# Local attention heads from the third chunk on: two at a time in plain float32 in place of one at a time with split operands

## The chip, the cores and the metric

The kernel runs on one core of a Trainium2 chip. TensorE (PE, with its weight loads as PEld) multiplies matrices, VectorE (DVE), ScalarE (ACT) and GpSimd (POOL) work on elements, SyncE (SP) issues transfers. The metric is the device time of one execution in microseconds, as a median over runs.

## The reference

Eight batches of eight heads, 576 positions, head size 64. Heads 0 to 3 attend to the last 32 positions, heads 4 to 7 to positions of the same remainder modulo 32. The result, heads side by side, goes through two dense layers with a squared ReLU between them. All of it is float32.

```python
def _attn_ref(q, k, v) -> np.ndarray:
    ...
    scores = scale * np.matmul(q, k.transpose(0, 1, 3, 2))
    ...
    mask_local = (rel >= 0) & (rel < stride)
    mask_strided = (rel >= 0) & (pos[None, :] % stride == pos[:, None] % stride)
    ...
    scores = np.where(masks[None, :, :, :], scores, -1000000000.0)
    scores = scores - np.max(scores, axis=-1, keepdims=True)
    attn = np.exp(scores)
    attn = attn / (np.sum(attn, axis=-1, keepdims=True) + 1e-09)
    return np.matmul(attn, v).astype(np.float32)

def _moe_ref(x, w_in, w_out) -> np.ndarray:
    h = np.maximum(x @ w_in, 0.0)
    return (h * h @ w_out).astype(np.float32)
```

Here x is 4608 x 512, `w_in` 512 x 2048 and `w_out` 2048 x 512.

## The kernel before

**Chunks and the MLP.** The 4608 tokens go in 12 chunks of 384. In each chunk the MLP runs over 16 tiles of the hidden dimension (slots). `up` (L466) does twelve matmuls of 384 columns per slot (L476), ScalarE applies ReLU, square and a rounding to `gh`, VectorE makes the remainder `gl` (L490). `down` (L494) does nine matmuls of 512 columns per slot (L509) into three PSUM banks, two slots later than `up`. The MLP's operands are split: a value is a rounded part (`float32r`, one instruction a matmul) and the remainder that the rounding left, and three of the four products are summed. That split is what all names with `h`/`l`, `x` or two halves stand for.

**Attention of the next chunk.** While the MLP of chunk c runs, the attention of chunk c+1 is done beside it. The strided heads (`strided`, L401) are products on GpSimd and sums on VectorE, with no TensorE. The local heads use TensorE. The first two chunks (`NPLAIN`, chunks 0 and 1) do them in pairs with `pe_pair` (L295) in plain float32: scores at L325 with 64 rows for each head, head 0 on partitions 0 to 63 and head 1 on 64 to 127; output at L381 with 64 output partitions for each head. Chunk 1's pairs lie among chunk 0's MLP matmuls. From the third chunk on, `pe_head` (L199) does one head at a time:

- loads: queries and keys, twice over on 128 partitions (L214), and values (L215);
- splits: rounded keys and queries on ScalarE (L220, L222), remainders on GpSimd (L221, L223);
- scores: four windows of 96 queries by 128 keys, one matmul of 256 columns each (L237), a column for a key and one for its remainder; the remainder's half and the mask are added on VectorE (L241), and the minimum is taken with the other half (L229);
- exponentials with row sums on ScalarE (L246), reciprocals on VectorE (L247, L248), scaling on ScalarE (L251) or, for the last head, on GpSimd (L254);
- probabilities transposed in blocks of 32 on VectorE into `p_t` (L262) and split (L270 to L272), values split (L257, L258);
- output: four matmuls of 192 columns on 128 x 128 weights (L283), whose parts are summed on ScalarE and VectorE (L286 to L288), then split into the MLP's operands `xlh` and `xll` (L290, L291).

PSUM banks 3 and 4 are taken in turn for scores and outputs.

**What sets the order.** TensorE's order is written out. For every two slots (a step, `j // 2` from 0 to 7) `plan[step]` (L569) names the heads that go one stage on before the two `up`s, between `up`s and `down`s, and after them; `take` (L580) advances the generators, and ties the matmuls behind the last ones with `issue_after`. The loads for the head 0 and 1 of a chunk and the split of head 0 come at slot 14 of the chunk before (L689). On the other engines and in SP's queue of transfers a scheduler orders the instructions by its own simulated times, with the program's order as the priority. A tile of a pool with `bufs=1` is written only when the tile before it in that place is no longer read.

Of the kernel before, what the change touches and what calls it, by code (L numbers as in the profile page):

```python
# [7 lines left out]
F32 = mybir.dt.float32  # L8
F32R = mybir.dt.float32r
BF16 = mybir.dt.bfloat16  # L10
U32 = mybir.dt.uint32
AF = mybir.ActivationFunctionType
ALU = mybir.AluOpType
AX = mybir.AxisListType
PSUM = bass.MemoryType.PSUM

B, H, S, D = 8, 8, 576, 64
HL = H // 2
STR = 32
# [3 lines left out]
P = 128  # L23
TC = 384
WP = 512
NCHUNK = NT // TC
NFT = DF // P
NTT = TC // P
QC = 96
NW = TC // QC  # L30
KW = QC + STR
KC = TC + 2 * STR
CI = TC // STR
SCALE = 1.0 / 8.0
# [3 lines left out]
NPLAIN = 2  # L38
# [11 lines left out]
def f32(ap):  # L50
    return ap.bitcast(F32)
# [32 lines left out]


@with_exitstack
def attn_moe(ctx: ExitStack, tc, qk_l, v_l, qk_d, v_d, qk_p, v_p, f_s, q_s, k_s, v_s, w_in, w_out, masks, eye, out):
    nc = tc.nc
    pool = lambda name, bufs, **kw: ctx.enter_context(tc.tile_pool(name=name, bufs=bufs, **kw))
    const = pool("const", 1)  # L90
# [5 lines left out]
    lraw = pool("lraw", 2)  # L96
    lpool = pool("lpool", 2)
    small = pool("small", 3)
# [3 lines left out]
    def psum(i, nm):  # L102

        return ps.tile([P, 512], F32, name=nm, tag=f"ps{i}")

    turn = iter(range(10000))

    mask_sb = const.tile([P, 4, P], F32, name="mask_sb")
    ident = const.tile([P, P], F32, name="ident")
# [3 lines left out]
    p_t = [const.tile([P, NW, QC], F32, name=f"p_t{i}") for i in range(2)]  # L113
# [82 lines left out]
        return xt[c]  # L196


    def pe_head(c, h):  # L199
        u = f"{c}_{h}"  # L200

        def bank(nm):
            return psum(3 + next(turn) % 2, f"{nm}{u}")

        def buf(pl, nm, n, tag, **kw):
            return pl.tile([P, n], F32, name=f"{nm}{u}", tag=tag, **kw)

        qk, vp = buf(lraw, "qk", TC + KC, "qk"), buf(lraw, "v", NW * D, "v")
        e = buf(lpool, "e", 512, "e")
        qr, kr = qk[:, :TC], qk[:, TC:]  # L210
        vr = vp.rearrange("p (w d) -> p w d", d=D)
        kw, wins = KW, [(at, 0 if qc == 0 else 1) for _, qc, at in windows(c)]
        nk = wins[-1][0] + KW
        nc.sync.dma_start(out=qk[:, : TC + nk], in_=qk_l[c, h, :, : TC + nk])  # L214
        last["s"] = nc.sync.dma_start(out=vp, in_=v_l[c, h])  # L215
        yield

        qx = lpool.tile([P, TC], F32R, name=f"qx{u}", tag="qh", bufs=1)
        kx = lpool.tile([P, 2, KC], F32R, name=f"kx{u}", tag="kx", bufs=1)
        nc.scalar.copy(kx[:, 0, :nk], kr[:, :nk])  # L220
        nc.gpsimd.tensor_sub(kx[:, 1, :nk], kr[:, :nk], f32(kx[:, 0, :nk]))  # L221
        nc.scalar.copy(qx, qr)  # L222
        nc.gpsimd.tensor_sub(qx[D:], qr[D:], f32(qx[D:]))  # L223
        yield
        nmax = small.tile([P, 2 * NW], F32, name=f"nm{u}", tag="nm")
        ssum = sums[h % 3]
        rs = small.tile([P, 2 * NW], F32, name=f"rs{u}", tag="rs")[:, :NW]
        cut = lambda w: slice(w * kw, (w + 1) * kw)
        reduce = lambda w, src, m: nc.vector.tensor_tensor_reduce(  # L229
            out=e[:QC, cut(w)], in0=src, in1=m, scale=-SCALE, scalar=3.0e38,  # L230
            op0=ALU.add, op1=ALU.min, accum_out=nmax[:QC, w : w + 1],
        )
        for a in range(0, NW, 2):
            s_ps = bank(f"s{a}")
            for w in (a, a + 1):
                k0 = wins[w][0]
                last["mm"] = nc.tensor.matmul(s_ps[:QC, 256 * (w - a) : 256 * (w - a + 1)], qx[:, w * QC : (w + 1) * QC], kx[:, :, k0 : k0 + kw], start=True, stop=True)  # L237
            sv = s_ps[:QC].rearrange("p (w t k) -> p w t k", w=2, t=2)
            m = wins[a][1]
            ev = e[:QC, a * kw : (a + 2) * kw].rearrange("p (w k) -> p w k", w=2)  # L240
            nc.vector.tensor_add(ev, sv[:, :, 1, :], mask_sb[:QC, m : m + 2, :])  # L241
            for w in (a, a + 1):
                reduce(w, sv[:, w - a, 0, :], e[:QC, cut(w)])
        yield
        for w in range(NW):
            nc.scalar.activation(e[:QC, cut(w)], e[:QC, cut(w)], AF.Exp, bias=nmax[:QC, w : w + 1], scale=-1.0, accum_out=ssum[:QC, w, :1])  # L246
        nc.vector.tensor_reduce(out=rs[:QC], in_=ssum[:QC, :NW], op=ALU.add, axis=AX.X)  # L247
        nc.vector.reciprocal(rs[:QC], rs[:QC])  # L248
        if h != HL - 1:
            for w in range(NW):  # L250
                nc.scalar.mul(e[:QC, cut(w)], e[:QC, cut(w)], rs[:QC, w : w + 1])  # L251
        else:
            ew = e[:QC, : NW * kw].rearrange("p (w k) -> p w k", k=kw)
            last["g"] = nc.gpsimd.tensor_mul(ew, ew, rs[:QC].unsqueeze(2).broadcast_to([QC, NW, kw]))  # L254
        yield
        vx = lpool.tile([P, NW, 2, D], F32R, name=f"vx{u}", tag="vx", bufs=1)
        nc.scalar.copy(vx[:, :, 0, :], vr)  # L257
        nc.gpsimd.tensor_sub(vx[:, :, 1, :], vr, f32(vx[:, :, 0, :]))  # L258
        pt = p_t[h % 2]
        for r in range(QC // STR):  # L260
            for k in (r, r + 1):
                nc.vector.transpose(  # L262
                    out=pt[STR * k : STR * (k + 1), :, STR * r : STR * (r + 1)],
                    in_=e.rearrange("p (w k) -> p w k", k=KW)[STR * r : STR * (r + 1), :, STR * k : STR * (k + 1)],
                )
        src = pt.rearrange("p w q -> p (w q)")
        px = lpool.tile([P, 2, TC], F32R, name=f"px{u}", tag="px")

        o_ps = bank("o0")
        nc.scalar.copy(o_ps[:, :TC], src)  # L270
        nc.scalar.copy(px[:, 0, :], src)
        nc.vector.tensor_sub(px[:, 1, :], o_ps[:, :TC], f32(px[:, 0, :]))  # L272
        yield
        x = x_tiles(c)
        par, hp = D * (h % 2), h // 2

        src = e[par : par + D, :TC]
        for a in range(0, NW, 2):
            if a:
                o_ps = bank(f"o{a}")  # L280
            for w in (a, a + 1):
                sl = slice(w * QC, (w + 1) * QC)
                last["mm"] = nc.tensor.matmul(o_ps[:, 2 * QC * (w - a) : 2 * QC * (w - a + 1)], vx[:, w].rearrange("p t d -> p (t d)"), px[:, :, sl], start=True, stop=True)  # L283
            ov = o_ps[:, : 4 * QC].rearrange("p (w t q) -> p w t q", w=2, t=2)
            part = src[:, a * QC : (a + 2) * QC].rearrange("p (w q) -> p w q", w=2)
            nc.scalar.copy(part, ov[D:, :, 0, :])  # L286
            nc.vector.tensor_add(part, ov[:D, :, 1, :], part)
            nc.vector.tensor_add(part, ov[:D, :, 0, :], part)  # L288
        dst = [x["l", s][par : par + D, hp, :] for s in "hl"]
        last["a"] = nc.scalar.copy(dst[0], src)  # L290
        last["g"] = nc.gpsimd.tensor_sub(dst[1], src, f32(dst[0]))  # L291
        yield


# [265 lines left out]
    def local(c):  # L560
# [7 lines left out]
    heads = {}  # L568
    plan = {  # L569
        0: ("", "0", "01"),  # L570
        1: ("", "1", "012"),
        2: ("", "0", "123"),
        3: ("", "1", ""),
        4: ("2", "", "23"),
        5: ("3", "", "23"),
        6: ("2", "", "3"),
        7: ("3", "", ""),
    }

    def take(c, which):  # L580

        if NPLAIN <= c < NCHUNK:
            for h in map(int, which):
                if (c, h) not in heads:
                    heads[c, h] = pe_head(c, h)
                with ExitStack() as st:
                    for i in (last["pe"], *(weights_end.values() if c == NPLAIN else ())):
                        st.enter_context(tc.issue_after(i.ins))
                    last.pop("mm", None)
                    next(heads[c, h])  # L590
                    last["pe"] = last.get("mm", last["pe"])
# [63 lines left out]
    for s in range(NS + 2):  # L655
# [30 lines left out]
                for t in p_t:  # L686
                    nc.gpsimd.memset(t, 0.0)
        if j == NFT - 2:
            take(c + 2, "010")  # L689
        if c + 1 < NCHUNK and s >= LATER:  # L690
            j0 = LATER if c == 0 else 0
            if j == j0:
# [17 lines left out]
                run(st)  # L710


_NAMES = ["qk_l", "v_l", "qk_d", "v_d", "qk_p", "v_p", "f_s", "q_s", "k_s", "v_s", "w_in", "w_out", "masks", "eye"]


def _layout(q, k, v, moe_w_in, moe_w_out):
# [2 lines left out]
    asc = np.ascontiguousarray  # L719
    a = {}  # L720

    twice = lambda t: asc(np.concatenate([t, t], axis=-2))
    pad = ((0, 0), (0, 0), (STR, 0), (0, 0))
    rows = lambda t, c: np.concatenate([t[b, :, SEG * g : SEG * (g + 1)] for b, g in SEGS[c]], axis=1)
    ql = np.stack([rows(q[:, :HL], c).transpose(0, 2, 1) for c in range(NCHUNK)])
# [3 lines left out]
    for c in range(NCHUNK):  # L729
        for w, (b, qc, at) in enumerate(windows(c)):  # L730
            kl[c, :, :, at : at + KW] = kp[b, :, QC * qc : QC * qc + KW].transpose(0, 2, 1)
            vl[c, :, :, w] = vp[b, :, QC * qc : QC * qc + KW]
    a["qk_l"], a["v_l"] = twice(np.concatenate([ql, kl], axis=3)), vl.reshape(NCHUNK, HL, KW, NW * D)

    two = lambda t: asc(t.reshape(t.shape[0], 2, 2, *t.shape[2:]).transpose(0, 1, 3, 2, 4))
    a["qk_d"] = asc(np.concatenate([ql, kl], axis=3)[:NPLAIN]).reshape(NPLAIN, 2, P, TC + KC)
    a["v_d"] = two(vl[:NPLAIN].reshape(NPLAIN, HL, KW, NW * D)).reshape(NPLAIN, 2, KW, 2 * NW * D)

    by_r = lambda t: rows(t[:, HL:], 0).reshape(HL, 2, SI, STR, D).transpose(0, 1, 3, 2, 4).reshape(HL, TC, D)
    a["qk_p"] = asc(np.concatenate([by_r(t).transpose(0, 2, 1) for t in (q, k)], axis=2)).reshape(2, P, 2 * TC)  # L740
# [46 lines left out]
```

## Time and profile before

The median of three runs is 880.01 us (879.94 to 880.58).

| of the profiled execution | |
|---|---|
| span from the first to the last instruction | 877.8 us |
| median of the runs, less that span | 2.2 us |
| TensorE busy | 867.9 us (99%), 4787 matmul records |
| weight loads busy | 788.9 us (90%) |
| VectorE busy | 640.3 us (73%), 1900 |
| ScalarE busy | 571.4 us (65%), 1506 |
| GpSimd busy | 672.2 us (77%), 718 |
| bytes moved by transfers | 71.42 MB |

The profiled execution's own time is told as its span; the 2.2 us above it are what the runs' median has more. A row of a group names the line, the engine, the operation, the tiles (out<-in), the shapes and the count, then busy time, mean nanoseconds of one, and the engine's idle time before them with what ended it. The ends of matmuls are modelled and overlap the next, so distances between starts are read, not lengths. A timeline row is the start, the length and the group, with idle time before it in brackets.

### The profile page before, as it was taken

The numbers are of one execution on the slowest core, as the hardware profiler recorded it, in microseconds if no ns is written. First come the engines' busy times: TensorE is split into PE (matmuls) and PEld (weight loads), VectorE is DVE, ScalarE is ACT, GpSimd is POOL, SyncE is SP. The second block draws the span as 40 slices with busy tenths as digits, with TensorE's granted clock in tenths as the row PEclk, the third lists the DMA queues.
The fourth block names the chain that finished last, engine by engine and source line by source line (L and its number), as shares of the span: only waits on it lengthen the run. The fifth ranks groups of instructions, "written<-read, shape, count | busy, mean of one in ns | idle before, by whom it ended". The sixth has DMA issues, their size and how long they took to land.

```text
span 877.8 us, 14934 instructions
## 1 busy us (share of the span) xinstructions
PE 867.9 (99%) x4787; PEld 788.9 (90%) x4787; DVE 640.3 (73%) x1900; ACT 571.4 (65%) x1506; POOL 672.2 (77%) x718
## 2 busy tenths in 40 slices
PE   8999999999999999999999999999999999999997
PEld 7788899999999999999989898989898989999996
DVE  5796587797787887878878779878778787883111
ACT  6998776586576666657756758657666665664332
POOL 3689778877978989888988978996998899782000
PEclk9999999999999999999999999999999999999999
DMA  9963531223123023112102302312031021000000
GB/s 351 363 212 95 178 95 46 85 84 114 32 86 103 27 89 103 44 62 87 58 9 80 116 13 77 100 32 75 31 103 58 29 71 62 7 0 15 23 1 37
DMA packets 26799, 71.42 MB, mean 81 GB/s; under 512 B 2976, under 2 KB 8736, under 8 KB 25184
## 3 DMA queue, kind: packets, MB, share of 16 engines
q1 hardware_dynamic: 26432, 70.14, 24.1%
q8 instruction: 38, 0.62, 0.3%
q14 instruction: 41, 0.34, 0.1%
q10 hardware_dynamic: 288, 0.33, 0.1%
HBM read 61.01 MB, written 9.44 MB: 80 GB/s over the span
## 4 chain that ended last, share of the span: by engine, by line
PE 95%; ACT 2%; POOL 1%; issue 0%; DVE 0%; DVEq 0%; POOLq 0%; ACTq 0%
PE h L476 45%; PE y L509 45%; PE s L237 2%; PE o L283 2%; ACT b L353 1%; PE w_ps L606 1%; PE b L325 1%; POOL w L173 1%; ACT raw L154 0%; ACT z L166 0%; POOL pq L426 0%; ACT w L172 0%; PE b L381 0%; ACT xsh L396 0%; PE b L369 0%
## 5 line engine op out<-in xcount | busy, mean ns | idle before, releaser
L509 PE MATMUL y<-w,gh 128*128 128x512 f32 x1152 | 357.9, 391 | 0.5 <-POOL w L173 0.5
L509 PEld LDWEIGHTS y<-w,gh 128*128 128x128 f32 x1152 | 212.7, 188 | 40.5 <-POOL w L173 0.8
L476 PE MATMUL h<-xlh,w 128*128 128x384 f32 x768 | 229.1, 339 | 1.3 <-ACT xlh L396 0.6
L448 POOL TENSOR_TENSOR pp<-vs,sc 128x448 f32<-128x448 f32 (+10 forms) x192 | 190.0, 1014 | 48.8 <-DVE qs L449 23.0
L476 PE MATMUL h<-xsh,w 128*128 128x384 f32 x768 | 226.4, 335 | 0.3 <-POOL w L173 0.3
L509 PE MATMUL y<-w,gl 128*128 128x512 f32 x576 | 225.2, 392 | 0.0
L426 POOL TENSOR_TENSOR pq<-ks,qs 128x512 f32<-128x512 f32 (+2 forms) x192 | 197.7, 1050 | 18.8 <-DVE sc L427 13.3
L490 DVE TENSOR_TENSOR gl<-h,gh 128x384 fp32r<-128x384 f32 x192 | 105.5, 550 | 80.9 <-ACT gh L489 79.8
L489 ACT CAST gh<-h 128x384 fp32r<-128x384 f32 x192 | 91.8, 478 | 104.3 <-PE y L509 103.3
L487 ACT ACTIVATE h<-h 128x384 f32<-128x384 f32 x176 | 83.1, 472 | 109.8 <-PE h L476 109.3
L427 DVE TENSOR_REDUCE sc<-pq 128x8 f32<-128x512 f32 (+4 forms) x228 | 119.7, 534 | 45.1 <-POOL pq L426 41.9
L476 PEld LDWEIGHTS h<-xlh,w 128*128 128x128 f32 x768 | 141.3, 188 | 4.9 <-ACT w L172 0.9
L476 PEld LDWEIGHTS h<-xsh,w 128*128 128x128 f32 x768 | 141.3, 188 | 1.1 <-POOL w L173 0.6
L476 PE MATMUL h<-xll,w 128*128 128x384 f32 x384 | 129.0, 336 | 0.0
L509 PEld LDWEIGHTS y<-w,gl 128*128 128x128 f32 x576 | 108.1, 188 | 22.9
L476 PE MATMUL h<-xsl,w 128*128 128x384 f32 x384 | 128.4, 334 | 0.0
L449 DVE TENSOR_REDUCE qs<-pp 128x64 f32<-128x448 f32 (+11 forms) x192 | 106.4, 562 | 27.3 <-POOL pp L448 25.5
L488 ACT ACTIVATE h<-h 128x384 f32<-128x384 f32 x176 | 83.3, 473 | 3.6
L262 DVE STREAM_TRANSPOSE p_t<-e 32x128 f32<-32x128 f32 x240 | 72.3, 301 | 11.2 <-ACT e L251 6.6
L476 PEld LDWEIGHTS h<-xll,w 128*128 128x128 f32 x384 | 72.2, 188 | 2.4 <-DVE xll L397 0.3
L476 PEld LDWEIGHTS h<-xsl,w 128*128 128x128 f32 x384 | 72.1, 188 | 0.2
L246 ACT ACTIVATE e<-e,nm 96x128 f32<-96x128 f32 x160 | 62.5, 392 | 10.1 <-DVE nm L229 8.7
(101 smaller groups left out, 1076.7 us busy)
## 6 DMA issues: line engine op xcount, KB each, us to landing
qk<-qk_l SPq DMA_DIRECT2D x24, 400.0 KB, 3.2
y<-ysb SPq DMA_DIRECT2D x36, 256.0 KB, 3.5
raw<-w_in SPq DMA_DIRECT2D x7, 1024.0 KB, 10.9
qk<-qk_l SPq DMA_DIRECT2D x16, 416.0 KB, 3.6
vs<-v_s SPq DMA_DIRECT2D x10, 576.0 KB, 3.9
raw<-w_out SPq DMA_DIRECT2D x5, 1024.0 KB, 12.6
v<-v_l SPq DMA_DIRECT2D x40, 128.0 KB, 2.1
ks<-k_s SPq DMA_DIRECT2D x8, 576.0 KB, 3.8
```

Of the source, the lines that this page charges most:

```text
L246: nc.scalar.activation(e[:QC, cut(w)], e[:QC, cut(w)], AF.Exp, bias=nmax[:QC, w : w + 1], scale=-1.0, accum_out=ssum[:QC, w, :1])
L262: nc.vector.transpose(out=pt[STR * k : STR * (k + 1), :, STR * r : STR * (r + 1)], in_=e.rearrange("p (w k) -> p w k", k=KW)[STR * r : STR ...
L426: nc.gpsimd.tensor_mul(pv, kt[:, a : a + m, :], qt[:, i - i0 : i - i0 + 1, :].broadcast_to([P, m, D]))
L427: nc.vector.tensor_reduce(out=sc[:, i - i0, a : a + m], in_=pv, op=ALU.add, axis=AX.X)
L448: nc.gpsimd.tensor_mul(pv, vt[:, a : a + nd, :n], sc[:, il : il + 1, :n].broadcast_to([P, nd, n]))
L449: nc.vector.tensor_reduce(out=ot[:, il, a : a + nd], in_=pv, op=ALU.add, axis=AX.X)
L476: done = nc.tensor.matmul(ph[:, :TC], w[:, wsl], xx, start=n == 0, stop=n == 11)
L487: nc.scalar.activation(g, g, AF.Relu)
L488: nc.scalar.activation(g, g, AF.Square)
L489: last["gh"] = nc.scalar.copy(gh, g)
L490: nc.vector.tensor_sub(gl, g, f32(gh))
L509: done = nc.tensor.matmul(y_ps[c][t], g[:, sl], w[:, wsl], start=j == 0 and k == 0, stop=j == NFT - 1 and k == 2)
```

## The change

`pe_head` is replaced by `pair`, which takes two heads. Queries and keys come from the array that `pe_pair` reads, with one head on each half of the partitions, and now reaches over all chunks. Nothing is split ahead of the multiplications. Scores are eight float32 matmuls of 64 rows and 128 columns, the heads in turn, into banks 3 and 4; the mask is added in the minimum itself, which reads PSUM. Both heads' exponentials, scaling (head 0 on ScalarE, head 1 on GpSimd) and transposes follow, then eight float32 output matmuls into one bank, the heads in turn on the two halves of the output partitions. ScalarE rounds that bank to `xlh`, VectorE makes `xll`. The values of a pair have a single buffer (`vx`). The plan has a pair's five stages in place of a head's six.

```diff
-    def pe_head(c, h):
...
+    def pair(c, pr):
...
+        qk, vr = buf(lraw, "qk", TC + KC, "qk"), buf(lpool, "v", 2 * NW * D, "vx", bufs=1)
+        nc.sync.dma_start(out=qk[:, : TC + nk], in_=qk_d[c, pr, :, : TC + nk])
+        last["s"] = nc.sync.dma_start(out=vr, in_=v_d[c, pr])
+        yield
...
+        ss = sums[pr]
+        s_ps = [psum(3 + h, f"s{h}{u}") for h in range(2)]
         for w in range(NW):
+            k0 = TC + wins[w][0]
+            for h in range(2):
+                rows = slice(D * h, D * (h + 1))
+                last["mm"] = nc.tensor.matmul(s_ps[h][:QC, w * kw : (w + 1) * kw], qk[rows, w * QC : (w + 1) * QC], qk[rows, k0 : k0 + kw], start=True, stop=True)
+        for h in range(2):
             for w in range(NW):
+                nc.vector.tensor_tensor_reduce(
+                    out=e4[h][:, w], in0=s_ps[h][:QC, w * kw : (w + 1) * kw], in1=mask_sb[:QC, wins[w][1], :], scale=-SCALE, scalar=3.0e38,
+                    op0=ALU.add, op1=ALU.min, accum_out=nm[:QC, h, w : w + 1],
                 )
+        yield
+        for h in range(2):
+            for w in range(NW):
+                nc.scalar.activation(e4[h][:, w], e4[h][:, w], AF.Exp, bias=nm[:QC, h, w : w + 1], scale=-1.0, accum_out=ss[:QC, NW * h + w, :1])
+            part = ss[:QC, NW * h : NW * (h + 1)]
+            nc.vector.tensor_reduce(out=rs[:QC, h], in_=part, op=ALU.add, axis=AX.X)
+            nc.vector.reciprocal(rs[:QC, h], rs[:QC, h])
+            if h == 0:
+                for w in range(NW):
+                    nc.scalar.mul(e4[h][:, w], e4[h][:, w], rs[:QC, h, w : w + 1])
+            else:
+                last["g"] = nc.gpsimd.tensor_mul(e4[h], e4[h], rs[:QC, h].unsqueeze(2).broadcast_to([QC, NW, kw]))
+        yield
+        for h in range(2):
+            ev = es[h].rearrange("p (w k) -> p w k", k=kw)
+            for r in range(QC // STR):
+                for k in (r, r + 1):
+                    nc.vector.transpose(
+                        out=p_t[h][STR * k : STR * (k + 1), :, STR * r : STR * (r + 1)],
+                        in_=ev[STR * r : STR * (r + 1), :, STR * k : STR * (k + 1)],
+                    )
         yield
         x = x_tiles(c)
+        v4 = vr.rearrange("p (h w d) -> p h w d", h=2, w=NW)
+        o = psum(3 + pr, f"o{u}")
+        for w in range(NW):
+            for h in range(2):
+                last["mm"] = nc.tensor.matmul(o[D * h : D * (h + 1), w * QC : (w + 1) * QC], v4[:kw, h, w], p_t[h][:, w], start=True, stop=True)
+        last["a"] = nc.scalar.copy(x["l", "h"][:, pr, :], o[:, :TC])
+        nc.vector.tensor_sub(x["l", "l"][:, pr, :], o[:, :TC], f32(x["l", "h"][:, pr, :]))
         yield
...
         0: ("", "0", "01"),
-        1: ("", "1", "012"),
-        2: ("", "0", "123"),
-        3: ("", "1", ""),
-        4: ("2", "", "23"),
-        5: ("3", "", "23"),
-        6: ("2", "", "3"),
-        7: ("3", "", ""),
+        1: ("", "", "0"),
+        2: ("", "0", ""),
+        3: ("", "", ""),
+        4: ("1", "", "1"),
+        5: ("", "", "1"),
+        6: ("1", "", ""),
+        7: ("", "", ""),
...
-            take(c + 2, "010")
+            take(c + 2, "0")
...
-    a["qk_l"], a["v_l"] = twice(np.concatenate([ql, kl], axis=3)), vl.reshape(NCHUNK, HL, KW, NW * D)
...
+    a["qk_d"] = asc(np.concatenate([ql, kl], axis=3)).reshape(NCHUNK, 2, P, TC + KC)
+    a["v_d"] = two(vl.reshape(NCHUNK, HL, KW, NW * D)).reshape(NCHUNK, 2, KW, 2 * NW * D)
```

More of the change, by code (lines that the diff above doesn't have):

```diff
@@ L86, in attn_moe @@
 @with_exitstack
-def attn_moe(ctx: ExitStack, tc, qk_l, v_l, qk_d, v_d, qk_p, v_p, f_s, q_s, k_s, v_s, w_in, w_out, masks, eye, out):
+def attn_moe(ctx: ExitStack, tc, qk_d, v_d, qk_p, v_p, f_s, q_s, k_s, v_s, w_in, w_out, masks, eye, out):
     nc = tc.nc
@@ L104, in psum @@
         return ps.tile([P, 512], F32, name=nm, tag=f"ps{i}")
-    turn = iter(range(10000))
     mask_sb = const.tile([P, 4, P], F32, name="mask_sb")
@@ L196, in x_tiles @@
         return xt[c]
-    def pe_head(c, h):
-        u = f"{c}_{h}"
-        def bank(nm):
-            return psum(3 + next(turn) % 2, f"{nm}{u}")
+    def pair(c, pr):
+        u = f"{c}_{pr}"
         def buf(pl, nm, n, tag, **kw):
             return pl.tile([P, n], F32, name=f"{nm}{u}", tag=tag, **kw)
[L208 to L211, printed above, removed]
@@ L212, in pe_head @@
         kw, wins = KW, [(at, 0 if qc == 0 else 1) for _, qc, at in windows(c)]
         nk = wins[-1][0] + KW
-        nc.sync.dma_start(out=qk[:, : TC + nk], in_=qk_l[c, h, :, : TC + nk])
-        last["s"] = nc.sync.dma_start(out=vp, in_=v_l[c, h])
+        qk, vr = buf(lraw, "qk", TC + KC, "qk"), buf(lpool, "v", 2 * NW * D, "vx", bufs=1)
+        nc.sync.dma_start(out=qk[:, : TC + nk], in_=qk_d[c, pr, :, : TC + nk])
+        last["s"] = nc.sync.dma_start(out=vr, in_=v_d[c, pr])
         yield
-        qx = lpool.tile([P, TC], F32R, name=f"qx{u}", tag="qh", bufs=1)
@@ L219, in pe_head @@
[L219 to L223, printed above, removed]
-        yield
[L225 to L243, printed above, removed]
@@ L244, in pe_head @@
-        yield
[L245 to L272, printed above, removed]
+        es = [buf(lpool, f"e{h}", NW * KW, "e") for h in range(2)]
+        e4 = [e.rearrange("p (w k) -> p w k", k=kw)[:QC] for e in es]
+        nm = small.tile([P, 2, NW], F32, name=f"nm{u}", tag="nm")
@@ new lines, in pair @@
+        rs = small.tile([P, 2, NW], F32, name=f"rs{u}", tag="rs")
+        ss = sums[pr]
[11 more added lines that the diff above has]
+                )
@@ new lines, in pair @@
+        yield
+        for h in range(2):
[5 more added lines that the diff above has]
+            if h == 0:
+                for w in range(NW):
+                    nc.scalar.mul(e4[h][:, w], e4[h][:, w], rs[:QC, h, w : w + 1])
+            else:
+                last["g"] = nc.gpsimd.tensor_mul(e4[h], e4[h], rs[:QC, h].unsqueeze(2).broadcast_to([QC, NW, kw]))
@@ L273, in pe_head @@
+        yield
+        for h in range(2):
[5 more added lines that the diff above has]
+                        in_=ev[STR * r : STR * (r + 1), :, STR * k : STR * (k + 1)],
+                    )
         yield
         x = x_tiles(c)
-        par, hp = D * (h % 2), h // 2
@@ L277, in pe_head @@
[L277 to L288, printed above, removed]
@@ L289, in pe_head @@
-        dst = [x["l", s][par : par + D, hp, :] for s in "hl"]
-        last["a"] = nc.scalar.copy(dst[0], src)
-        last["g"] = nc.gpsimd.tensor_sub(dst[1], src, f32(dst[0]))
+        v4 = vr.rearrange("p (h w d) -> p h w d", h=2, w=NW)
+        o = psum(3 + pr, f"o{u}")
+        for w in range(NW):
+            for h in range(2):
+                last["mm"] = nc.tensor.matmul(o[D * h : D * (h + 1), w * QC : (w + 1) * QC], v4[:kw, h, w], p_t[h][:, w], start=True, stop=True)
+        last["a"] = nc.scalar.copy(x["l", "h"][:, pr, :], o[:, :TC])
@@ L584, in take @@
                 if (c, h) not in heads:
-                    heads[c, h] = pe_head(c, h)
+                    heads[c, h] = pair(c, h)
                 with ExitStack() as st:
@@ L710, in attn_moe @@
                 run(st)
-_NAMES = ["qk_l", "v_l", "qk_d", "v_d", "qk_p", "v_p", "f_s", "q_s", "k_s", "v_s", "w_in", "w_out", "masks", "eye"]
+_NAMES = ["qk_d", "v_d", "qk_p", "v_p", "f_s", "q_s", "k_s", "v_s", "w_in", "w_out", "masks", "eye"]
 def _layout(q, k, v, moe_w_in, moe_w_out):
@@ L720, in _layout @@
     a = {}
-    twice = lambda t: asc(np.concatenate([t, t], axis=-2))
     pad = ((0, 0), (0, 0), (STR, 0), (0, 0))
@@ L732, in _layout @@
             vl[c, :, :, w] = vp[b, :, QC * qc : QC * qc + KW]
-    a["qk_l"], a["v_l"] = twice(np.concatenate([ql, kl], axis=3)), vl.reshape(NCHUNK, HL, KW, NW * D)
     two = lambda t: asc(t.reshape(t.shape[0], 2, 2, *t.shape[2:]).transpose(0, 1, 3, 2, 4))
-    a["qk_d"] = asc(np.concatenate([ql, kl], axis=3)[:NPLAIN]).reshape(NPLAIN, 2, P, TC + KC)
-    a["v_d"] = two(vl[:NPLAIN].reshape(NPLAIN, HL, KW, NW * D)).reshape(NPLAIN, 2, KW, 2 * NW * D)
+    a["qk_d"] = asc(np.concatenate([ql, kl], axis=3)).reshape(NCHUNK, 2, P, TC + KC)
+    a["v_d"] = two(vl.reshape(NCHUNK, HL, KW, NW * D)).reshape(NCHUNK, 2, KW, 2 * NW * D)
     by_r = lambda t: rows(t[:, HL:], 0).reshape(HL, 2, SI, STR, D).transpose(0, 1, 3, 2, 4).reshape(HL, TC, D)
```

## The prediction

> **What bounds the kernel now.** I read the busy shares first, then the chain of waits, then the chain by pieces, then single stretches of TensorE.
>
> ```profile
> span 877.8 us, 14934 instructions
> PE 867.9 (99%) x4787; PEld 788.9 (90%) x4787; DVE 640.3 (73%) x1900; ACT 571.4 (65%) x1506; POOL 672.2 (77%) x718
> PE 95%; ACT 2%; POOL 1%; issue 0%; DVE 0%; DVEq 0%; POOLq 0%; ACTq 0%
> PE h L476 45%; PE y L509 45%; PE s L237 2%; PE o L283 2%; ACT b L353 1%; PE w_ps L606 1%; PE b L325 1%; POOL w L173 1%; ACT raw L154 0%; ACT z L166 0%; POOL pq L426 0%; ACT w L172 0%; PE b L381 0%; ACT xsh L396 0%; PE b L369 0%
> ```
>
> TensorE is 99% of the span and 95% of the chain that ended last. The work of this change stands in it as L237 (scores) and L283 (output). The stretches below, with TensorE first and then the weight load, VectorE, ScalarE and GpSimd, are one middle chunk and the last chunk, which has no heads in it:
>
> ```profile
> 487.79:557.85 70.06, 70.06 (x370) 64.08 (x369) 54.50 (x160) 45.78 (x126) 60.53 (x63) 1.00 0.17 52
> 802.57:865.00 62.43, 62.43 (x320) 57.19 (x320) 9.56 (x17) 21.87 (x47) 0.00 (x0) 1.00 0.04 13
> ```
>
> In the middle chunk TensorE has no idle time (70.06 of 70.06 us) at a granted clock of 1.00; VectorE, ScalarE and GpSimd all have some. So only TensorE instructions, or a new wait of TensorE, can move the end. The chain by pieces (start, length, line, count) shows how a chunk is made up:
>
> ```profile
> 487.79 4.16 PE h L476 x24
> 491.95 4.13 PE y L509 x18
> 496.08 0.47 PE s L237 x4
> ...
> 557.85 4.16 PE h L476 x24
> ...
> 802.57 4.18 PE h L476 x24
> 806.75 4.12 PE y L509 x18
> 810.88 4.18 PE h L476 x24
> ```
>
> A step of two slots is 24 matmuls of the first layer and 18 of the second; without heads it takes 810.88 - 802.57 = 8.31 us, so one matmul of `up` holds TensorE 4.18/24 = 0.174 us, one of `down` 4.12/18 = 0.229. A chunk of eight such steps is 66.5 us, the middle chunk took 557.85 - 487.79 = 70.06, so its four heads cost 3.58 us of TensorE, 0.89 a head.
>
> **What the change does to TensorE.** Ten chunks (the third to the twelfth) carry it, so 40 heads become 20 pairs. First what goes. The timeline of TensorE around one group of old scores and one of old output:
>
> ```profile
> 556.98 0.40 PE L509 MATMUL y<-w,gl 128*128 128x512 f32 x1
> 557.21 0.63 PE L237 MATMUL s<-kx,qx 128*96 128x256 f32 x4
> ...
> 557.86 0.34 PE L476 MATMUL h<-xll,w 128*128 128x384 f32 x1
> ...
> 574.50 0.39 PE L509 MATMUL y<-w,gl 128*128 128x512 f32 x1
> 574.73 0.59 PE L283 MATMUL o<-px,vx 128*128 128x192 f32 x4
> ...
> 575.53 0.52 PE L476 MATMUL h<-xlh,w 128*128 128x384 f32 x2
> ```
>
> I price a group by start times: from the last ordinary matmul before it to one after it, less the ordinary slots in between. Scores: 557.86 - 556.98 - 0.229 - 0.174 = 0.48 us. Output: 575.53 - 574.50 - 0.229 - 2 x 0.174 = 0.45 us. Two heads: 2 x 0.93 = 1.86 us. (Four heads make 3.72 against the 3.58 from the chunk's length; I keep both sums.)
>
> What comes has been run already: `pe_pair` does the first two chunks' local heads in plain float32 with the same shapes (L325, L381), and the second chunk's lie among the same MLP matmuls:
>
> ```profile
> 62.58 0.34 PE L476 MATMUL h<-xsl,w 128*128 128x384 f32 x1
> 62.85 1.11 PE L325 MATMUL b<-qk 64*96 64x128 f32 x8
> 63.89 0.50 PE L509 MATMUL y<-w,gh 128*128 128x512 f32 x1
> 64.22 0.51 PE L476 MATMUL h<-xsh,w 128*128 128x384 f32 x2
> ...
> 86.64 0.40 PE L509 MATMUL y<-w,gh 128*128 128x512 f32 x1
> 86.96 0.88 PE L381 MATMUL b<-pt,v 128*64 128x96 f32 x16
> 87.77 0.50 PE L509 MATMUL y<-w,gl 128*128 128x512 f32 x1
> 88.11 0.40 PE L509 MATMUL y<-w,gh 128*128 128x512 f32 x1
> 88.36 0.40 PE L509 MATMUL y<-w,gl 128*128 128x512 f32 x1
> ```
>
> ```profile
> 6.82 2.67 PE L325 MATMUL b<-qk 64*96 64x128 f32 x48
> ```
>
> ```profile
> L325 PE MATMUL b<-qk x96: 243/269/347, 6.8 to 70.3; 64*96 64x128 f32 x64, 64*96 64x96 f32 x32
> ```
>
> Each float32 matmul of the program is two instructions: a head's four scores are 8 records, a pair's eight output matmuls 16.
>
> - Output of a pair, 16 records: 88.36 - 86.64 - 3 x 0.229 = 1.03 us. The same form and order of heads as in the change.
> - Scores of one head, 8 records one after another: 64.22 - 62.58 - 0.174 - 0.229 = 1.24 us.
> - Scores of a pair as the change orders them, head 0 and head 1 in turn: in the first chunk's 48 records, which alternate so (32 of 128 columns, 16 of 96, so 5632 columns), 2.67 less a last matmul of 0.243 is 2.43 us, 0.43 ns a column. 16 records of 128 columns stream in 0.88 us. One head's 8 records took 63.89 - 62.85 = 1.04 us, so alone they step about twice as slowly; at 0.86 ns a column they too make 0.88. So two heads share the time of one, and what is left of its 1.24 us, 0.36, is the cost of entering and leaving. I take 0.88 + 0.36 = 1.24 us for a pair; the lower bound is no edge at all, 0.88, the upper no overlap, 2.12.
> - Output likewise: 16 x 96 columns stream in 0.66 us, the edge is 0.37.
>
> The edge is seen in the weight loads:
>
> ```profile
> 62.40 0.19 PEld L476 LDWEIGHTS h<-xsl,w 128*128 128x128 f32 x1
> 62.85 0.24 PEld L325 LDWEIGHTS b<-qk 64*96 64x96 f32 x2 [0.26 <-issue]
> ...
> 556.76 0.19 PEld L509 LDWEIGHTS y<-w,gl 128*128 128x128 f32 x1
> 556.98 0.39 PEld L237 LDWEIGHTS s<-kx,qx 128*96 128x96 f32 x2
> ```
>
> The load for the old scores starts at 556.98, a matmul ahead; that for 64 rows starts only at 62.85, with its own matmul, after 0.26 us in which nothing that the profile shows held it. [...]
>
> **The sum.** A pair: 1.24 + 1.03 = 2.27 us for 1.86, so +0.41; twenty pairs +8.2 us. From the chunk's length: 2 x 2.27 = 4.54 for 3.58, +0.96 in each of ten chunks, +9.6 us. Between the two: +9 us. In the profiled execution the span goes from 877.8 to about 886.8 us; the median shown, 880.01 (879.94 to 880.58), lies 2.2 us above that span, so the time is 889.0 us.
>
> **What I cost at nothing.** All splits (L220 to L223, L257, L258, L270 to L272, the adds of L241, L287 and L288) leave ScalarE, VectorE and GpSimd. TensorE waits for none of them in the middle chunk, so their going is worth 0; at most the steps beside them would run at the bare rate of 8.31, and 4.16 + 4.13 = 8.29 is that already. The halved number of loads is worth 0 too: the DMA share is 0.17 in that chunk. What the cover hides: the pair's work between scores and output must fit in two steps, 2 x 8.31 = 16.6 us, or TensorE waits. The fourth head of a chunk before (its first add and its transposes on VectorE), and the costs of what a second head adds:
>
> ```profile
> 426.30 0.42 DVE L241 TENSOR_TENSOR e<-s,mask_sb 96x256 f32<-96x256 f32 x1
> 434.37 1.88 DVE L262 STREAM_TRANSPOSE p_t<-e 32x128 f32<-32x128 f32 x6 [0.16 <-POOL e L254]
> ```
>
> ```profile
> L246 ACT ACTIVATE e<-e,nm 96x128 f32<-96x128 f32 x160 | 62.5, 392 | 10.1 <-DVE nm L229 8.7
> L251 ACT ACTIVATE e<-e,rs 96x128 f32<-96x128 f32 x120 | 38.6, 392 | 4.6 <-DVE rs L248 4.3
> L330 DVE CUSTOM_DVE_ANT_0 e<-b,mask_sb 96x128 f32<-96x128 f32 x32 | 7.1, 281 | 8.0 <-PE b L325 8.0
> ```
>
> From 426.30 to 434.37 + 1.88 = 436.25 are 9.95 us. A second head adds four exponentials (4 x 0.392), four scalings (4 x 0.392), six transposes (1.88) and four minima (4 x 0.281, less the two adds of 0.42 that go): 5.3 us end to end, 15.2 in all, 1.4 us inside the 16.6. Much of it will overlap. The value load of the second pair waits in the SP queue for the first pair's output (one buffer, `vx`), about 22 us into the chunk (two steps, an `up` and a group of scores); it is needed at step 6, some 29 us on. Strided loads (L413 to L415) that stand behind it in that queue would wait with it; they feed a chunk's worth of GpSimd work, and for the range I take that as part of rival 2.
>
> **The rivals.**
>
> 1. *Not slower: the change of tiling is not paid, or paid once.* Place: entry and exit of the 40 new groups. Without it a pair is 0.88 + 0.66 = 1.54 us for 1.86: -0.32 x 20 = -6.4 us, 873.6. It decides as soon as the two edges of a pair sum to less than 0.32 us; with exactly that the time stays at 880. Against it: 0.36 and 0.37 us are in the rows above, between the same MLP matmuls. For it: only that those rows are few, and that in the scores the heads did not alternate there. 8%.
> 2. *TensorE waits for the probabilities.* If the pair's chain is 1 us later than 16.6 us, each of 20 pairs pays 1 us: 889 + 20 = 909. For it: only 1.4 us of margin in the bound, and an in-order VectorE queue shared with the strided products. Against it: the bound adds everything end to end, and splits vanish from all three engines. 10%.
> 3. *The two heads' scores do not overlap next to the MLP.* 2.12 for 1.24 us, +0.88 x 20 = +17.6: 906.6. Against it: the 48 records in 2.67 us. 5%. [...]
>
> **How the numbers follow.** The forecast, 889.0, has 77%; its own range, from both sums with 1 us around, is 887 to 891. Low end 885.5: edges a quarter cheaper (0.18 x 20 = 3.6 us less). High end 896: a wait of 0.35 us for every pair (7 us). Together with part of rivals 2 and 3 this leaves out under 2 in 10. About 0.2% (1.8 us) is what a measurement of this kernel can tell from no change. Faster by more takes most of rival 1: 0.05; within it, the rest of it (edges about halved) and a last hundredth of the forecast's own tail: 0.04; slower: 0.91.
>
> **What would show it.** TensorE 4787 - 320 + 640 = 5107 records. Each middle chunk about 71.0 us for 70.06; scores 1.24 and output 1.03 us a pair by start times; weight loads at their heads not ahead of their matmuls. GpSimd, ScalarE and VectorE busy far less, with nothing gained. Wrong if the middle chunk is at or under 70 us (edges), or over 72 with idle time of TensorE ahead of the output matmuls, ended by VectorE (rival 2).

## The result and the profile after

The changed kernel takes 888.0 us (median of 4 runs, 887.47 to 888.65) for 879.98 us before on the same chip (879.43 to 880.58): a ratio of 1.0089, 95% interval [1.0075, 1.0103]. It is slower by 8.0 us; forecast were 9 us more, 889.0. One execution of a later run, the output over full columns, took 1787.25 us, twice its others, and is left out of that run's median.

First the profile's page of the changed kernel, its span, the engines and the chain that ended last:

```profile
span 886.9 us, 14492 instructions
PE 877.0 (99%) x5107; PEld 783.0 (88%) x5107; DVE 557.0 (63%) x1640; ACT 444.0 (50%) x1166; POOL 530.1 (60%) x568
PE 95%; ACT 2%; POOL 1%; issue 0%; DVE 0%; DVEq 0%; POOLq 0%; ACTq 0%
```

VectorE lost 83 us of work (640.3 to 557.0), ScalarE 127 (571.4 to 444.0), GpSimd 142 (672.2 to 530.1). None of it came back in the time. TensorE is still 99% of the span, with the 5107 matmul records that were foretold.

Then a middle chunk of the changed kernel: the busy times of the stretch (TensorE, weight load, VectorE, ScalarE, GpSimd, then the granted clock), and the chain by pieces.

```profile
493.64:564.54 70.90, 70.90 (x401) 63.41 (x401) 53.67 (x148) 33.41 (x93) 58.17 (x60) 1.00 0.20 62
```

```profile
492.59 1.05 PE s L219 x16
493.64 4.36 PE h L440 x24
498.00 4.12 PE y L473 x18
502.12 4.18 PE h L440 x24
506.31 4.12 PE y L473 x18
510.43 0.81 PE o L253 x16
511.24 4.36 PE h L440 x24
...
564.54 4.36 PE h L440 x24
```

TensorE has no idle time in the chunk; the chunk is longer by 564.54 - 493.64 - 70.06 = 0.84 us, ten times that is 8.4 us. The first `up` after a new group takes 4.36 us in place of 4.18: the way back to the full tiling shows there (behind scores over full rows, in the fourth run, it takes 4.17).

The two new groups on TensorE, with one weight load:

```profile
492.20 0.39 PE L473 MATMUL y<-w,gl 128*128 128x512 f32 x1
492.52 1.12 PE L219 MATMUL s<-qk 64*96 64x128 f32 x16
...
494.03 0.51 PE L440 MATMUL h<-xlh,w 128*128 128x384 f32 x2
...
510.04 0.39 PE L473 MATMUL y<-w,gl 128*128 128x512 f32 x1
510.36 0.88 PE L253 MATMUL o<-p_t,v 128*64 128x96 f32 x16
...
511.63 0.51 PE L440 MATMUL h<-xlh,w 128*128 128x384 f32 x2
```

```profile
492.52 0.47 PEld L219 LDWEIGHTS s<-qk 64*96 64x96 f32 x8 [0.35 <-PE y L473]
```

Priced as in the prediction (0.229 a slot of `down`, two of 0.174 of `up`): scores 494.03 - 492.20 - 0.229 - 0.348 = 1.25 us, output 511.63 - 510.04 - 0.229 - 0.348 = 1.01 us. The first weight load of the scores starts with its matmul, not ahead of it, after 0.35 us without a load. The bracket names the matmul before it as what the load waited for; whether that wait or the tiling holds it is settled by the run with the scores over full rows.

One part of the 9.1 us between the two spans is not the change's. The first scores of the program start here at 7.66 us, before at 6.82; ahead of them are only the warm-up matmuls, and that start lies anywhere from 6.37 to 7.83 us in the profiles of this study. The rest, 9.1 - 0.84 = 8.3 us, is the ten chunks.

### The profile page after: what moved, and what is told of

It reads as the page before. It is cut to its first block, busy times and chain, and to the rows that moved or that the text cites. A ratio compares the mean times of both kernels' runs of the same rounds, so it can differ in the third digit from the quotient of the medians.

```text
span 886.9 us, 14492 instructions
## 1 busy us (share of the span) xinstructions
PE 877.0 (99%) x5107; PEld 783.0 (88%) x5107; DVE 557.0 (63%) x1640; ACT 444.0 (50%) x1166; POOL 530.1 (60%) x568
## 4 chain that ended last, share of the span: by engine, by line
PE 95%; ACT 2%; POOL 1%; issue 0%; DVE 0%; DVEq 0%; POOLq 0%; ACTq 0%
PE h L440 45%; PE y L473 45%; PE s L219 2%; PE o L253 2%; ACT b L317 1%; PE w_ps L570 1%; PE b L289 1%; POOL w L171 1%; ACT raw L152 0%; ACT z L164 0%; POOL pq L390 0%; ACT w L170 0%; PE b L345 0%; ACT xsh L360 0%; PE b L333 0%
## 5 line engine op out<-in xcount | busy, mean ns | idle before, releaser
L473 PE MATMUL y<-w,gl 128*128 128x512 f32 x576 | 222.5, 392 | 0.0
```

The lines of the kernel that those rows point to most:

```text
L473: done = nc.tensor.matmul(y_ps[c][t], g[:, sl], w[:, wsl], start=j == 0 and k == 0, stop=j == NFT - 1 and k == 2)
```

## The experiments

Each is an edit of the changed kernel, except the eighth. Ratios are to the kernel before, run beside it; the changed kernel stands at 1.0089. A group is priced as above; 0.577 us stands for the ordinary matmuls between its two ends (0.229 + 2 x 0.174).

**Heads apart.**

```diff
-        for w in range(NW):
-            k0 = TC + wins[w][0]
-            for h in range(2):
-                rows = slice(D * h, D * (h + 1))
+        for h in range(2):
+            rows = slice(D * h, D * (h + 1))
+            for w in range(NW):
+                k0 = TC + wins[w][0]
```

> Scores of head 0 first and then of head 1, nothing else changed. Theory (the two heads' scores share TensorE's time because they stand in different halves of its rows): 16 records no longer overlap, 16 x 0.109 = 1.75 us for 0.87 of streaming, +0.87 us a pair, 20 pairs: +17.4 us, 905.4 us for the changed kernel's 888.0. Rival (the time of a group goes by its number of instructions, in whatever order): no change, 888.0.

Measured: 898.45 us, ratio 1.0199 [1.0184, 1.0214]. Slower, so the rival falls, but by 10 us and not by 17. The timeline of TensorE in this kernel:

```profile
569.52 0.39 PE L473 MATMUL y<-w,gl 128*128 128x512 f32 x1
569.84 1.63 PE L219 MATMUL s<-qk 64*96 64x128 f32 x16
...
571.86 0.33 PE L440 MATMUL h<-xlh,w 128*128 128x384 f32 x1
```

The group costs 571.86 - 569.52 - 0.229 - 2 x 0.174 = 1.76 us for 1.25, and 20 x 0.51 = 10.3 us is the whole difference. The starts of its 16 records (us after 569, the times of the trace) show why it is not 2.12:

```
0.841 1.028 1.137 1.246 1.355 | 1.361 1.465 1.548 1.574 1.657 1.683 | 1.766 1.875 1.985 2.094 2.203
```

In the program's order on TensorE all of head 0 stands ahead of head 1; at its step of 109 ns head 0's eight records end with the one at 1.683. Yet the sixth start lies 6 ns after the fifth, where records of one head step by 109 ns: head 1 begins while three of head 0's eight are still to come. So even here three records of each head overlap. The full price of no overlap is in the fourth run.

**Scores in halves.**

```diff
         for w in range(NW):
+            if w == NW // 2:
+                yield
...
-        0: ("", "0", "01"),
+        0: ("0", "0", "01"),
...
-        3: ("", "", ""),
+        3: ("", "1", ""),
```

> The eight score matmuls of a pair in two groups of four, with the 24 matmuls of one up (pair 0) or the 18 of one down (pair 1) in between. Theory (each group pays 0.37 us for entering and leaving another tiling): 20 groups more, +7.4 us, 895.4 us. Rival (the tiled matmuls themselves are slow, a group has no fixed price): no change, 888.0.

Measured: 896.62 us, ratio 1.0177 [1.0162, 1.0192].

```profile
497.80 0.39 PE L475 MATMUL y<-w,gl 128*128 128x512 f32 x1
498.11 0.68 PE L221 MATMUL s<-qk 64*96 64x128 f32 x8
...
499.18 0.51 PE L442 MATMUL h<-xlh,w 128*128 128x384 f32 x2
```

A half costs 499.18 - 497.80 - 0.577 = 0.80 us; two make 1.61 for 1.25, so each group more costs 0.36. The work and the records are the same, with one more way in and out: the fixed price stands.

**Outputs together.** Both pairs' outputs at step 6, in one group.

```diff
-        qk, vr = buf(lraw, "qk", TC + KC, "qk"), buf(lpool, "v", 2 * NW * D, "vx", bufs=1)
+        qk, vr = buf(lraw, "qk", TC + KC, "qk"), buf(lpool, "v", 2 * NW * D, ("vx", "kx")[pr], bufs=1)
...
+            if pr and not p_u:
+                t = lpool.tile([P, 2, NW, QC], F32, name="p_u", tag="px")
+                nc.gpsimd.memset(t, 0.0)
+                p_u.extend(t[:, i] for i in range(2))
+            pt = (p_t, p_u)[pr][h]
...
-        2: ("", "0", ""),
+        2: ("", "", ""),
...
-        6: ("1", "", ""),
+        6: ("01", "", ""),
```

> The output matmuls of both pairs of a chunk as one group at step 6, with own buffers for the second pair's probabilities and values. Theory (a fixed price for each group): ten groups fewer at 0.37 us, -3.7 us, 884.3 us, still slower than the 880.0 of the kernel before. Rival (no fixed price): no change, 888.0.

Measured: 884.28 us, ratio 1.0039 [1.0025, 1.0053], as the theory has it.

```profile
506.45 0.39 PE L480 MATMUL y<-w,gl 128*128 128x512 f32 x1
506.76 0.88 PE L260 MATMUL o<-p_t,v 128*64 128x96 f32 x16
507.48 0.83 PE L260 MATMUL o<-p_u,v 128*64 128x96 f32 x16
...
508.69 0.51 PE L447 MATMUL h<-xlh,w 128*128 128x384 f32 x2
```

32 records cost 508.69 - 506.45 - 0.577 = 1.66 us, where two groups of 16 cost 2.02: 0.36 us less.

**Scores over full rows.**

```diff
-                ... qk[rows, w * QC : (w + 1) * QC], qk[rows, k0 : k0 + kw], start=True, stop=True)
+                ... qk[:, w * QC : (w + 1) * QC], qk[:, k0 : k0 + kw], start=True, stop=True)
```

> Each score matmul contracts over all 128 partitions in place of one head's 64; it leaves out that the heads are kept apart, so each score is the sum of both heads'. Instructions, columns and order as in the changed kernel. No overlap is left: 16 x 0.109 = 1.75 us of streaming. Theory (the fixed price is for the change of tiling): it falls from 0.37 to the 0.12 us that the full-size float32 transposes of chunk 0 leave, a pair 1.87 for 1.25 us, +12.4 us, 900.4 us, and the first weight load comes ahead of its matmul. Rival (the fixed price belongs to plain float32): 1.75 + 0.37, +17.4 us, 905.4 us.

Measured: 898.39 us, ratio 1.0199 [1.0184, 1.0214].

```profile
568.54 0.40 PE L473 MATMUL y<-w,gl 128*128 128x512 f32 x1
568.78 1.91 PE L219 MATMUL s<-qk 128*96 128x128 f32 x16
...
570.88 0.51 PE L440 MATMUL h<-xlh,w 128*128 128x384 f32 x2
```

```profile
568.55 0.72 PEld L219 LDWEIGHTS s<-qk 128*96 128x96 f32 x5
```

The group costs 570.88 - 568.54 - 0.577 = 1.76 us. Of it 16 x 0.109 = 1.74 are streaming, so next to nothing is left for the way in and out, less than the 0.12 that I had allowed, and the first weight load starts at 568.55, a matmul ahead. It waits for the same semaphores as in the changed kernel, in all 20 groups; there it starts 0.27 to 0.32 us after the start of the last ordinary matmul, here within 0.004 us of it (568.55 and 568.54 in the group shown). So no wait of the program holds it back in the changed kernel. Plain float32 over the full array pays next to no fixed price here (1.76 - 1.74 = 0.02 us, for 0.36 in the tiled form); the price belongs to the change of tiling. Without overlap the eight score matmuls stream for 1.74 us, twice the 0.87.

**Output over full columns.**

```diff
+        vb = lpool.tile([P, NW, 2, D], F32, name=f"vb{u}", tag="vb", bufs=1)
+        nc.gpsimd.tensor_copy(vb, vr.rearrange("p (h w d) -> p w h d", h=2, w=NW))
...
-                last["mm"] = nc.tensor.matmul(o[D * h : D * (h + 1), w * QC : (w + 1) * QC], v4[:kw, h, w], p_t[h][:, w], start=True, stop=True)
+                last["mm"] = nc.tensor.matmul(os[h][:, w * QC : (w + 1) * QC], vb[:kw, w].rearrange("p h d -> p (h d)"), p_t[h][:, w], start=True, stop=True)
```

> Output matmuls with both heads' values as 128 weight columns, each head into a bank of its own, of which half the partitions are used; a copy on GpSimd puts the values side by side. Theory (the fixed price is for the change of tiling, and tiled columns let two heads overlap): 16 x 0.0825 = 1.32 us of streaming plus 0.12 us, 1.44 for 1.01 us a pair, +8.5 us, 896.5 us. Rival (the fixed price belongs to plain float32): 1.32 + 0.37 = 1.69, +13.5 us, 901.5 us.

Measured: 904.4 us (median of three executions), ratio 1.0274 [1.0253, 1.0294], above both numbers.

```profile
517.90 0.39 PE L477 MATMUL y<-w,gl 128*128 128x512 f32 x1
518.13 1.92 PE L255 MATMUL o<-p_t,vb 128*128 128x96 f32 x16
...
520.27 0.52 PE L444 MATMUL h<-xlh,w 128*128 128x384 f32 x2
```

The group costs 520.27 - 517.90 - 0.577 = 1.79 us. The way in is free again (518.13 is one slot of 0.229 after 517.90), but a record of 96 columns takes 0.110 us here, not the 0.0825 worked out from the tiled form (0.66 us for the 16 of a pair, two heads at a time). Of the 1.79 us, 16 x 0.110 = 1.76 are streaming, so next to no fixed price is left here either (0.03 us); the theory holds in that, and its term for the streaming was too small. What differs is the width of the weights, 128 columns for 64. A weight load of 128 columns takes 190 ns in the kernel before (L283), one of 64 columns 137 ns in the changed kernel (L253). That the load sets this step is the author's guess; no run shows it.

**Splits kept.** The old splits of both heads, into tiles that nobody reads, ahead of the minima.

```diff
+        for i in range(2):
...
+            nc.scalar.copy(kx[:, 0, :nk], qk[:, TC : TC + nk])
+            nc.gpsimd.tensor_sub(kx[:, 1, :nk], qk[:, TC : TC + nk], f32(kx[:, 0, :nk]))
+            nc.scalar.copy(qx, qk[:, :TC])
+            nc.gpsimd.tensor_sub(qx[D:], qk[D:, :TC], f32(qx[D:]))
+            nc.scalar.copy(vs[:, :, 0, :], vh)
+            nc.gpsimd.tensor_sub(vs[:, :, 1, :], vh, f32(vs[:, :, 0, :]))
```

> The changed kernel with the old splits of queries, keys and values done again for both heads, on ScalarE and GpSimd, into tiles that nobody reads: about 2.9 us of ScalarE and 5.7 us of GpSimd a pair. Theory (TensorE waits for neither, so taking the splits away was worth nothing): 888.0 us, within 1 us. Rival (their going gave part of a gain that the new matmuls ate): slower by 2 us or more.

Measured: 891.52 us, ratio 1.0124 [1.0109, 1.0139]: 3 us slower, by its number the rival. But from the third chunk on the chunks are as long as in the changed kernel (70.91 us from one chunk's first `up` to the next's in seven of nine, 70.94 and 71.23 in the others). Most of the loss lies in the second chunk, 74.83 us for 72.81, with one wait of TensorE:

```profile
151.66 0.44 PE L451 MATMUL h<-xlh,w 128*128 128x384 f32 x1 [1.56 <-DVE gl L465]
```

**Splits kept, later.** The same block moved behind the output, to try whether the wait came from its place.

> As the run with the old splits kept, but issued after the pair's output in place of ahead of its minima, so that they do not lie in the queues between scores and output. Theory (what that run lost was one wait of TensorE, made by where the splits stood and by nothing that the kernel before had): 888 us, within 1 us of the changed kernel. Rival (the load on ScalarE and GpSimd costs by itself): 890.5 us or more, as there.

Measured: 894.03 us, ratio 1.016 [1.0143, 1.0176]. My theory falls: moved away, the splits cost more. The rival in its plain form does not hold either. VectorE and TensorE of this kernel, and the granted clock (the 1.00 and the 0.54, the third number from the end of each stretch):

```profile
140.41 0.69 DVE L402 TENSOR_REDUCE sc<-pq 128x8 f32<-128x512 f32 x1 [0.74 <-POOL pq L401]
141.02 0.28 DVE L222 CUSTOM_DVE_ANT_0 e<-s,mask_sb 96x128 f32<-96x128 f32 x1
...
147.04 3.77 DVE L243 STREAM_TRANSPOSE p_t<-e 32x128 f32<-32x128 f32 x12 [1.23 <-ACT e L235]
...
150.99 0.55 DVE L465 TENSOR_TENSOR gl<-h,gh 128x384 fp32r<-128x384 f32 x1
```

```profile
151.59 0.47 PE L451 MATMUL h<-xlh,w 128*128 128x384 f32 x1 [2.69 <-DVE gl L465]
```

```profile
140.00:148.00 8.00, 8.00 (x42) 7.25 (x41) 5.44 (x30) 6.67 (x27) 5.80 (x7) 1.00 0.10 39
151.60:155.00 3.40, 3.40 (x11) 3.40 (x12) 1.42 (x5) 0.00 (x0) 2.42 (x3) 0.54 0.01 2
```

```profile
498.66 4.37 PE h L451 x24
...
569.57 4.36 PE h L451 x24
```

ScalarE ends the scaling late; VectorE waits 1.23 us for it, then does all twelve transposes of the pair in a row, 3.77 us, and only behind them the MLP's `gl`. `up` needs a PSUM bank that `gl` still reads. TensorE idles 2.69 us, and after that runs for 3.4 us at a clock of 0.54. In the changed kernel the same twelve transposes in the same chunk run 2.3 us earlier, and `up` does not wait:

```profile
139.44 0.28 DVE L222 CUSTOM_DVE_ANT_0 e<-s,mask_sb 96x128 f32<-96x128 f32 x1
...
144.72 3.77 DVE L243 STREAM_TRANSPOSE p_t<-e 32x128 f32<-32x128 f32 x12
148.52 0.56 DVE L454 TENSOR_TENSOR gl<-h,gh 128x384 fp32r<-128x384 f32 x1
```

Of these 2.3 us, 141.02 - 139.44 = 1.6 are there before ScalarE begins: the pair's minima stand on VectorE behind a strided sum (L402) that waited for GpSimd, and the chain of waits before it runs through GpSimd's part of the splits (642.0 us busy in this run for 530.1). Two split copies on ScalarE, one before the last exponential (144.46) and one before the scaling (145.31), make up about the rest.

A middle chunk with the late splits is 569.57 - 498.66 = 70.91 us, as without them; two of the nine are longer (71.24 and 71.88), and the second chunk takes 77.35 us for 72.81. So taking the splits away is worth nothing in most chunks, and their load costs where it delays a pair's twelve transposes past the MLP's turn. The kernel before, with such a load but six transposes at a time, had no such wait; whether the six are the reason was not tried.

**Output early.** The output of a pair one step after its scores in place of two.

```diff
-        0: ("", "0", "01"),
-        1: ("", "", "0"),
-        2: ("", "0", ""),
+        0: ("", "0", "001"),
+        1: ("", "0", ""),
+        2: ("", "", ""),
...
-        4: ("1", "", "1"),
-        5: ("", "", "1"),
-        6: ("1", "", ""),
+        4: ("1", "", "11"),
+        5: ("1", "", ""),
+        6: ("", "", ""),
```

> The output matmuls of each pair one step earlier, 8.3 us after its scores in place of 16.6. Theory (the pair's chain from the scores to the last transpose takes about 10.5 us, and only the distance of two steps hides it): TensorE waits 2 to 3 us a pair, +40 to +60 us, 928 to 948 us, with idle time of TensorE ahead of the output, ended by VectorE. Rival (the other engines bring the chain forward when it is needed earlier): under 5 us slower.

Measured: 927.85 us, ratio 1.0537 [1.0516, 1.0558]. TensorE's output, and who waited for whom:

```profile
L253 PE MATMUL o<-p_t,v 128*64 128x96 f32 x320 | 26.0, 263 | 26.2 <-DVE p_t L243 25.6
```

TensorE idles 25.6 us for the transposes, about 1.3 us a pair on the mean (the last four pairs hardly wait) and not the 2 to 3 of the theory. The time comes out just under the theory's low end (928) only because more was lost beside the idle time. In five stretches of 3.4 us TensorE has about half its clock (0.58 over 451.50 to 455.00, which takes in one of them), by an estimate some 5 x 3.4 x 0.5 = 8.5 us in all; what is left, about 6 us, was not taken apart. The two steps between scores and output are a cover that the change needs.

**Split scores, plain outputs.** By the experiments plain outputs pay the fixed price once a group, and the split scores, on the full array, pay next to none: their 4 x 256 columns at 0.174/384 us are 0.46 of the 0.48 us. So this run takes the kernel before with its scores, and all four heads' outputs in one plain float32 group at step 7:

```diff
-        vx = lpool.tile([P, NW, 2, D], F32R, name=f"vx{u}", tag="vx", bufs=1)
-        nc.scalar.copy(vx[:, :, 0, :], vr)
-        nc.gpsimd.tensor_sub(vx[:, :, 1, :], vr, f32(vx[:, :, 0, :]))
-        pt = p_t[h % 2]
+        pt = (*p_t, *p_u)[h]
...
+        for pr in range(2):
+            v4 = values[c, pr].rearrange("p (h w d) -> p h w d", h=2, w=NW)
+            o = psum(3 + pr, f"o{c}_{pr}")
+            for w in range(NW):
+                for i in range(2):
+                    last["mm"] = nc.tensor.matmul(o[D * i : D * (i + 1), w * QC : (w + 1) * QC], v4[:, i, w], (*p_t, *p_u)[2 * pr + i][:, w], start=True, stop=True)
...
-        2: ("", "0", "123"),
-        3: ("", "1", ""),
+        2: ("", "", "123"),
+        3: ("", "", ""),
...
-        6: ("2", "", "3"),
+        6: ("", "", "3"),
```

> The kernel before with its split scores (full tiling, 0.478 us of TensorE a head), and the changed kernel's plain float32 outputs, all four heads of a chunk as one group at step 7. Theory (a group of tiled outputs is 0.083 us for each two heads' record pair plus one fixed price; the group of 32 records took 1.667 us in the run with both pairs' outputs together): a chunk's heads take 4 x 0.478 + 1.667 = 3.58 us for the 4 x (0.478 + 0.449) = 3.71 of before, -0.13 us in each of ten chunks, 878.7 us beside 880.0, so faster than both, by 0.15%. Rival (leaving the full tiling costs more between split scores, or the later output of three heads makes TensorE wait at the chunk's end): 881 us or more.

Measured: 879.4 us (11 runs) for 880.33 us before (15 runs), ratio 0.9988 [0.9979, 0.9996].

```profile
486.99:556.95 69.96, 69.96 (x385) 63.52 (x385) 53.41 (x149) 38.20 (x105) 59.30 (x59) 1.00 0.22 66
```

A chunk is 69.96 us for 70.06. It is faster than the kernel before by about 1 us, a little less than the 1.3 of the sum, and so faster than both.

## Why the prediction was right

- *TensorE alone sets the end.* Right: 70.90 of 70.90 us busy, with 83 to 142 us of work gone from each other engine and no gain from it. The two runs with the splits kept show the limit of this: the load is free only while it does not delay VectorE past the MLP's turn.
- *Output 1.03 us, scores 1.24 us a pair.* Measured 1.01 and 1.25. That two heads in turn cost what one head cost in the second chunk held; it was worked out from the first chunk's 48 records.
- *The edge of 0.36 and 0.37 us.* Shown three ways: a group more (+0.36), a group fewer (-0.36), and the same float32 matmuls without tiling (0.02 us). So it is the change of tiling that costs, 0.36 us for the way there and back.
- *The sum.* The term that was off is the one from the chunk's length, +0.96 us a chunk (9.6 us in all): measured 0.84. It set a group's price by start times against a figure by chunk length, and those two differ by 0.14 us a chunk for the old heads (3.72 and 3.58). They differ for the new heads too: 2 x (1.25 + 1.01) = 4.52 by start times, 70.90 - 66.48 = 4.42 by length (66.48 us are eight steps without heads). Taken alike on both sides, start times give +0.80 and lengths +0.84 a chunk. By start times alone, +8.2 us, the forecast would have been 888.2. Why the two ways differ was not found.
- *Rival 1, no edge:* fell, by the same three runs. *Rival 3, no overlap:* the changed kernel shows 16 records in 1.12 us; undoing the alternation costs 10.3 us, not 17.6, since TensorE itself overlaps three records of each head.
- *Rival 2, a wait for the probabilities:* it did not come. The bound of 15.2 us was wide. From the first minimum to the end of the last transpose the changed kernel takes 502.31 + 1.87 - 493.98 = 10.2 us, of 16.6:

```profile
493.98 0.28 DVE L222 CUSTOM_DVE_ANT_0 e<-s,mask_sb 96x128 f32<-96x128 f32 x1
...
499.43 1.84 DVE L243 STREAM_TRANSPOSE p_t<-e 32x128 f32<-32x128 f32 x6
...
502.31 1.87 DVE L243 STREAM_TRANSPOSE p_t<-e 32x128 f32<-32x128 f32 x6
```

  That it is the distance of two steps which hides the chain is shown by the run with the output early, 40 us slower. The wait that does lie near is another one than I named: the MLP's `gl` behind twelve transposes.

## What to carry to other kernels

Price a group of small matmuls from start to start, with the ordinary matmuls on both sides, because a group in another tiling paid 0.36 us here on the way in and out, which the length of its own records does not show. When one engine has no idle time, count only its instructions: 83 to 142 us taken from three other engines were worth nothing here. Still look at what those engines release: late in its queue, one of them made the busy engine wait (VectorE's `gl`, 2.69 us with the late splits). If a group has a fixed price, make fewer and larger groups, and keep the cover that the work between them needs.

## What was not expected of the hardware

- TensorE started matmuls of the second half of its rows before three earlier ones of the first half (the run with heads apart): the first of them starts at 570.361, 6 ns after a record of the other head, where one head's records step by 109 ns.
- An idle stretch of TensorE of 2.69 us was followed by 3.4 us at a granted clock of 0.54, and that chunk became 4.5 us longer. One of 1.56 us (the run with the splits kept) was followed by a clock of 1.00:

```profile
151.60:155.00 3.40, 3.34 (x17) 3.13 (x18) 1.50 (x6) 0.92 (x2) 2.35 (x2) 1.00 0.01 2
```

  The length of the stretch does not decide it alone. In the run with the output early, 1.84 us of idle time left the clock at 1.00, and 1.74 us were followed by a slow stretch:

```profile
418.07 0.88 PE L253 MATMUL o<-p_t,v 128*64 128x96 f32 x14 [1.84 <-DVE p_t L243]
451.45 1.02 PE L253 MATMUL o<-p_t,v 128*64 128x96 f32 x14 [1.74 <-DVE p_t L243]
```

```profile
418.10:421.50 3.40, 3.40 (x25) 2.83 (x26) 2.47 (x5) 0.96 (x2) 2.84 (x3) 1.00 0.28 77
451.50:455.00 3.50, 3.50 (x22) 3.28 (x23) 2.96 (x6) 0.48 (x1) 2.89 (x3) 0.58 0.24 80
```

- A float32 record of 96 moving columns took 0.110 us with 128 weight columns (the run with the output over full columns), and two of them 0.081 us with 64 weight columns each (16 more records added 1.66 - 1.01 = 0.65 us in the run with the outputs together).
